# Two 128x64 column tiles in place of two zero-padded 128x128 matmuls for the last key tile of an attention kernel

## The chip, the cores and the metric

The kernel runs on one core of a Trainium2 chip. The metric is the device time of one execution in microseconds (us). A core has a matrix engine (PE, with its weight loads shown apart as PEld), a vector engine (DVE), an activation engine (ACT), a general engine (POOL), a queue engine (SP) and 16 DMA engines. A matmul on PE is two instructions: LDWEIGHTS puts the stationary operand into the 128x128 array, MATMUL streams the moving operand through it, one column after another, and writes PSUM.

## What is computed

Attention with RMS-normalized queries and keys, and then a layer-norm MLP with a residual. Eight batches, twelve heads, 448 tokens, head size 64:

```python
q_n, k_n = (rmsnorm(q, g_q), rmsnorm(k, g_k))
scores = scale * np.matmul(q_n, k_n.transpose(0, 1, 3, 2))
attn = np.exp(scores - np.max(scores, axis=-1, keepdims=True))
attn = attn / (np.sum(attn, axis=-1, keepdims=True) + 1e-09)
x = np.matmul(attn, v)            # 12 heads side by side: 768 columns
xn = (x - mu) / np.sqrt(var + 1e-06) * g_ln
out = x + np.maximum(xn @ w_ch1, 0.0) @ w_ch2     # 768 -> 3072 -> 768
```

## The kernel before

**Pairs and key tiles.** The kernel works on pairs of heads: 8 batches with 6 pairs each, 48 pairs. A head's 448 keys are three tiles of 128 and a rest of 64. For a pair that gives seven key tiles: tiles 0 to 2 are of the first head, 3 to 5 of the second, and tile 6 holds the last 64 keys of both heads. Scores are laid out with keys on the partitions and the 448 queries along the free dimension, so that their exponentials can serve at once as stationary operands of the product with V.

**The contraction.** A key is split into a high and a low half-precision part. Both stand along the contraction (64 rows high, 64 rows low, together 128), and the query is there twice. So every score matmul contracts over all 128 rows of the array, also that of tile 6.

**Scores** (`scores(p, i)`). For i below 6 one matmul (L351) loads 128 keys as weights and streams 448 query columns of that head. For tile 6 the transposed keys of a pair stand in a buffer `left` of 192 columns: 64 keys of the first head, 64 zeros, 64 keys of the second head. Two matmuls (L354, L355) write the same 128x448 tile of PSUM: the first takes columns 0 to 127 (keys of the first head and zeros) with the first head's queries, the second takes columns 64 to 191 (zeros and keys of the second head) with the second head's queries and adds to it. Then ACT takes the exponential of the whole tile (L357). Score tiles have two PSUM buffers (three in the later part).

**Values** (`values(p, i)`). Each exponential tile is used as weights, in four matmuls (three at L389, one at L391), over 65 columns of V (a column of ones gives the sum), or over 130 columns for tile 6. After tile 6, DVE divides and evacuates (`evac_o`, L404 to L411).

**The MLP** runs batch by batch, one batch behind the attention: `up` (L631, six matmuls of up to 512 columns for each of 24 hidden tiles, evacuated by ACT at L633) and `down` (L647, 24 matmuls of 384 columns for each output tile, evacuated by DVE at L651).

**The order.** Each engine executes its own list in order. For the first batch the order is a list by hand (`ORDER`: S3.6 is the scores of tile 6 of pair 3). Afterwards `run_rest` takes the chunks of the MLP of batch b and puts steps of the attention of batch b+1 between them in proportion to their cost, so that score, value and MLP matmuls alternate on PE. The order on PE, ACT, POOL and SP is as emitted; that on DVE is left to a scheduler in `run_rest`. Inputs are loaded ahead by DMAs; from the ninth load unit on the normalized keys and queries are transposed by DMA (L257 to L270), before that by PE (L312 to L329). The low part of the keys is made on DVE at L239.

**One other small tile.** Once, in the last batch, `flag` sums a check over the partitions with a matmul of one weight column in 32-bit floats (L760, tile psF, two passes). In the built program it is the only matmul of the kernel before that is marked as a tile smaller than 128x128: 128x32. It is emitted behind the third `up` of the last batch, between ordinary 128x128 matmuls.

Of the kernel before, what the change touches and what calls it, by code (L numbers as in the profile page):

```python
# [16 lines left out]
ts = bass.ts  # L17

B, H, S, D = 8, 12, 448, 64
# [56 lines left out]
class _Fast:  # L76
# [261 lines left out]
    def scores(self, p, i):  # L338

        nc = self.nc  # L340
        c = self.prs[p]
        q, left = c["q"], c["left"]
        if i == 0:
            c["E"] = self.p_e.tile([128, 7, S], FP16, tag="E", name="E")
        if p > UNIT_PAIR[DMA_UNIT] and (7 * p + i) % 3 == 2:
            ps = self.ps_tr.tile([128, 512], FP32, tag="tr", name="psS3")
        else:
            ps = self.ps_s.tile([128, 512], FP32, tag="psS", name="psS")
        if i < 6:
            h = i // 3  # L350
            nc.tensor.matmul(ps[:, 0:S], c["main"][:, ts(i, 128)], q[:, ts(h, S)],  # L351
                             start=True, stop=True)
        else:
            nc.tensor.matmul(ps[:, 0:S], left[:, 0:128], q[:, 0:S], start=True, stop=False)  # L354
            nc.tensor.matmul(ps[:, 0:S], left[:, 64:192], q[:, S:2 * S], start=False, stop=True)  # L355
        g = self.group(p, i)
        nc.scalar.activation(out=c["E"][:, i], in_=ps[:, 0:S], func=AFT.Exp,  # L357
                             scale=self.units[PAIR_UNIT[p][0]][3][:, g:g + 1], bias=EXP_BIAS)

        u = PAIR_UNIT[p][0]  # L360
        if i == 6 and UNIT_PAIR[u] == p and u > 4:
            self.least(u)
# [584 lines left out]
```

## Time and profile before

| what | value |
|---|---|
| median of three runs | 608.54 us (608.29 to 608.70) |
| span of the profiled execution, first to last instruction | 606.9 us |
| PE busy with matmuls | 579.4 us, 4500 recorded matmuls |
| mean granted TensorE clock | 0.996 |
| L354 and L355, 48 matmuls each | 17.2 and 17.1 us busy, 358 and 357 ns mean |
| L351, 288 matmuls of the same shape | 100.9 us busy, 358 ns mean |
| L760, its two passes | 0.2 us busy, 164 ns mean |

The profile comes from one execution. Matmuls are pipelined: a record of 0.35 us covers a matmul from its start until its last result is out, while the next one may start much earlier. What a matmul costs a busy PE is the distance from its start to the next start, which the timeline shows. "Idle before" is the time that an engine stood still before an instruction, with what ended it. The chain of waits is followed back from the last instruction of the program; a line's share of it is how much of the span that line itself set.

### The profile page before, as it was taken

The numbers are of one execution on the slowest core, as the hardware profiler recorded it, in microseconds if no ns is written. First come the engines' busy times: TensorE is split into PE (matmuls) and PEld (weight loads), VectorE is DVE, ScalarE is ACT, GpSimd is POOL, SyncE is SP. The second block draws the span as 40 slices with busy tenths as digits, with TensorE's granted clock in tenths as the row PEclk, the third lists the DMA queues.
The fourth block names the chain that finished last, engine by engine and source line by source line (L and its number), as shares of the span: only waits on it lengthen the run. The fifth ranks groups of instructions, "written<-read, shape, count | busy, mean of one in ns | idle before, by whom it ended". The sixth has DMA issues, their size and how long they took to land.

```text
span 606.9 us, 11525 instructions
## 1 busy us (share of the span) xinstructions
PE 579.4 (95%) x4500; PEld 346.4 (57%) x4500; DVE 287.1 (47%) x643; ACT 359.5 (59%) x673; POOL 190.1 (31%) x245
## 2 busy tenths in 40 slices
PE   2887999999999999999999999999999999999995
PEld 1555666655566666655566666655566666654564
DVE  5799567734256256715256255633356322530011
ACT  5996887268743697458753598538754377124200
POOL 3854432233541355332552345423412000000000
PEclk9899999999999999999999999999999999999999
DMA  8999999478954596747955485748733330030011
GB/s 225 275 192 200 214 225 187 103 211 83 149 157 107 89 136 154 174 133 90 126 129 127 114 123 141 188 120 124 125 74 68 92 62 1 31 100 0 1 53 57
DMA packets 130861, 75.29 MB, mean 124 GB/s; under 512 B 96656, under 2 KB 121040, under 8 KB 130800
## 3 DMA queue, kind: packets, MB, share of 16 engines
q1 hardware_dynamic: 114048, 45.12, 38.3%
q0 software_dynamic: 16080, 28.94, 22.1%
q8 instruction: 37, 0.61, 0.5%
q10 hardware_dynamic: 672, 0.43, 0.2%
q14 instruction: 24, 0.20, 0.1%
HBM read 52.36 MB, written 11.01 MB: 104 GB/s over the span
## 4 chain that ended last, share of the span: by engine, by line
PE 90%; DVE 2%; ACT 0%; issue 0%; DVEq 0%
PE psC L647 36%; PE psH L631 35%; PE psS L351 8%; PE oA L389 5%; PE oB L391 2%; PE psS L354 1%; PE psS L355 1%; PE tr L329 0%; PE tr L315 0%; PE psU L677 0%; DVE stat L555 0%; DVE xn L576 0%; DVE x L406 0%; DVE qU L334 0%; ACT E L357 0%
## 5 line engine op out<-in xcount | busy, mean ns | idle before, releaser
L631 PE MATMUL psH<-xnT,w 128*128 128x512 f16 (+1 forms) x1134 | 241.9, 353 | 0.0
L357 ACT ACTIVATE E<-psS,rr_all 128x448 f16<-128x448 f32 x336 | 207.6, 635 | 49.5 <-PE psS L351 44.3
L647 PE MATMUL psC<-w,hT 128*128 128x384 f16 (+1 forms) x1368 | 234.7, 323 | 0.0
L633 ACT ACTIVATE hT<-psH 128x512 f16<-128x512 f32 (+1 forms) x189 | 104.1, 551 | 124.3 <-PE psH L631 122.3
L647 PEld LDWEIGHTS <-hT 128*128 128x128 f16 x1368 | 127.8, 98 | 74.4
L631 PEld LDWEIGHTS <-w 128*128 128x128 f16 x1134 | 102.6, 98 | 80.5
L351 PE MATMUL psS<-qU,kU 128*128 128x448 f16 x288 | 100.9, 358 | 8.0 <-ACT E L357 5.3
L389 PEld LDWEIGHTS <-E 128*128 128x128 f16 x1008 | 71.2, 99 | 48.7 <-issue 4.1
L228 POOL TENSOR_TENSOR qkv<-qkv,gprod 128x896 f32<-128x896 f32 x21 | 43.7, 2080 | 95.3 <-issue 49.5
L389 PE MATMUL oA<-v,E 128*128 128x65 f16 x864 | 67.0, 194 | 0.1
L651 DVE SCALAR_TENSOR_TENSOR x<-psC,rs_all,x 128x384 f32<-128x384 f32 x48 | 28.9, 615 | 72.0 <-PE psC L647 71.5
L404 DVE RECIPROCAL rec_all<-oA 128x6 f32<-128x6 f32 x48 | 9.3, 193 | 94.0 <-PE oA L389 93.8
L391 PE MATMUL oB<-v,E 128*128 128x65 f16 x288 | 52.0, 194 | 0.1
L127 POOL DMA_DIRECT2D qkv<-in_k_dram x14 | 11.2, 799 | 129.8 <-ACT E L357 60.3
L217 DVE TENSOR_REDUCE ssq<-khl 128x14 f32<-128x896 f32 (+1 forms) x24 | 25.6, 1065 | 44.6 <-ACT khl L214 44.5
L351 PEld LDWEIGHTS <-kU 128*128 128x128 f16 x288 | 28.2, 99 | 25.8 <-issue 6.1
L217 DVE TENSOR_REDUCE ssq<-qn 128x14 f32<-128x896 f32 (+1 forms) x25 | 26.1, 1046 | 21.9 <-ACT qn L214 21.8
L67 DVE SCALAR_TENSOR_TENSOR qn<-qkv,rr_all 128x256 f16<-128x256 f32 (+1 forms) x72 | 26.3, 424 | 15.3 <-ACT rr_all L221 15.3
L391 PEld LDWEIGHTS <-E 128*128 128x128 f16 x336 | 32.7, 97 | 0.3 <-DVE xl L411 0.2
L239 DVE TENSOR_TENSOR khl<-qkv,khl 128x896 f16<-128x896 f32 x21 | 22.7, 1083 | 10.6 <-ACT khl L236 9.7
L406 DVE TENSOR_TENSOR x<-oA,rec_all 128x384 f32<-128x384 f32 x48 | 26.8, 558 | 1.5
L555 DVE BATCH_NORM_STATS2 stat<-x 128x6 f32<-128x256 f32 (+1 forms) x75 | 26.2, 404 | 0.6
(104 smaller groups left out, 448.4 us busy)
## 6 DMA issues: line engine op xcount, KB each, us to landing
out_dram<-x SPq DMA_DIRECT2D x20, 384.0 KB, 2.5
qkv<-in_k_dram POOLq DMA_DIRECT2D x14, 384.0 KB, 3.9
qkv<-in_q_dram POOLq DMA_DIRECT2D x14, 384.0 KB, 5.2
qkv<-in_v_dram POOLq DMA_DIRECT2D x14, 384.0 KB, 7.8
w<-in_moe_w_ch_dram POOLq DMA_DIRECT2D x3, 1536.0 KB, 12.6
w<-in_moe_w_ch_dram POOLq DMA_DIRECT2D x2, 2304.0 KB, 24.1
qkv<-in_k_dram SPq DMA_DIRECT2D x7, 384.0 KB, 6.6
qkv<-in_q_dram SPq DMA_DIRECT2D x7, 384.0 KB, 6.1
```

The costliest lines, as they stand in the source:

```text
L67: nc.vector.scalar_tensor_tensor(out=out, in0=x, scalar=8.0, in1=r.unsqueeze(2).broadcast_to([x.shape[0], g, D]), op0=ALU.mult, op1=ALU.mult)
L217: nc.vector.tensor_reduce(out=c["ssq"][:, n], in_=c["sq", n], axis=AX.X, op=ALU.add)
L228: (nc.vector if u in DVE_KG else nc.gpsimd).tensor_tensor(out=c["t"][1], in0=c["t"][1], in1=sh.gprod.unsqueeze(1).broadcast_to([128, g, D] ...
L351: nc.tensor.matmul(ps[:, 0:S], c["main"][:, ts(i, 128)], q[:, ts(h, S)], start=True, stop=True)
L357: nc.scalar.activation(out=c["E"][:, i], in_=ps[:, 0:S], func=AFT.Exp, scale=self.units[PAIR_UNIT[p][0]][3][:, g:g + 1], bias=EXP_BIAS)
L389: nc.tensor.matmul(oA[:, t, cs], E[:, i, ts(t, 128)], rhs, start=(i == 0 and t == 0), stop=(i == 6 and t == 2))
L391: nc.tensor.matmul(oB[:, cs], E[:, i, 320:448], rhs, start=(i == 0), stop=(i == 6))
L406: nc.vector.tensor_tensor(out=x[:, :, 128 * hp:128 * hp + 128].rearrange("p t (e d) -> p t e d", e=2), in0=oA[:, :, :, 0:D], in1=rec[:, 0: ...
L631: nc.tensor.matmul(ps[:, 0:N], sh.w1[:, dc, ts(f, 128)], xnT[:, dc, 0:N], start=(dc == 0), stop=(dc == NDC - 1))
L633: nc.scalar.activation(out=hT[:, f, 0:N], in_=ps[:, 0:N], func=AFT.Relu)
L647: nc.tensor.matmul(ps[:, 0:g[1]], hT[:, f, ts(t, 128)], sh.w2[:, f, cols], start=(f == 0), stop=(f == NFF - 1))
L651: nc.vector.scalar_tensor_tensor(out=x[:, cols], in0=ps[:, 0:g[1]], scalar=self.rs[:, b, t:t + 1], in1=x[:, cols], op0=ALU.mult, op1=ALU.add)
```

## The change

For tile 6 each head now has a matmul of its own with 64 weight columns. The first takes the 64 keys of the first head and writes partitions 0 to 63 of the PSUM tile; the second takes the 64 keys of the second head and writes partitions 64 to 127. Nothing accumulates, and the zeros in `left` are no longer read (they are still written).

```diff
         else:
-            nc.tensor.matmul(ps[:, 0:S], left[:, 0:128], q[:, 0:S], start=True, stop=False)
-            nc.tensor.matmul(ps[:, 0:S], left[:, 64:192], q[:, S:2 * S], start=False, stop=True)
+            for e in range(2):
+                nc.tensor.matmul(ps[64 * e:64 * e + 64, 0:S], left[:, 128 * e:128 * e + 64],
+                                 q[:, ts(e, S)], start=True, stop=True)
```

In the built program the two weight loads and the two matmuls of each pair are marked as tiles of 128x64 of the array, the first at column 0, the second at column 64; all other matmuls keep their marks. The lists of PE, ACT, POOL and SP hold the same instructions in the same order. On DVE the scheduler moves a few instructions: at three places in the stretch that it orders, the low part of a unit's keys (L239 of the kernel before) comes behind the evacuation of a pair (L404 to L411) and three statistics (L555) instead of ahead of them, and one evacuation of the MLP (L651) comes behind all of these; in a fourth place a small reduction (L366) comes two instructions later.

## The prediction, made before the changed kernel ran

> **What bounds the kernel now.** I read the page's busy times and chain first, then busy times by stage, then the chain by line.
>
> ```profile
> PE 579.4 (95%) x4500; PEld 346.4 (57%) x4500; DVE 287.1 (47%) x643; ACT 359.5 (59%) x673; POOL 190.1 (31%) x245
> ...
> PE 90%; DVE 2%; ACT 0%; issue 0%; DVEq 0%
> ```
>
> ```profile
> 0.00:58.00 58.00, 37.78 (x430) 25.75 (x431) 45.74 (x94) 44.73 (x86) 31.13 (x41) 0.97 0.98 232
> ...
> 120.00:520.00 400.00, 399.87 (x3045) 235.52 (x3043) 179.30 (x413) 255.70 (x477) 139.74 (x186) 1.00 0.61 119
> ```
>
> The first column after a stretch's length is PE. From 120 to 520 us PE is busy in 399.87 of 400 us at full clock; ACT, next, in 255.70. Only in the first 58 us does PE stand still for long (20 us). So a change of PE's work counts in full after 58 us, and in part before. Where are the edited matmuls?
>
> ```profile
> 0.00:58.00 58.00, 2.72 (x7) 0.77 (x7) 0.97 0.98 232
> 58.00:520.00 462.00, 14.45 (x41) 4.00 (x41) 1.00 0.66 126
> ```
>
> ```profile
> by line: PE psC L647 35.8%; PE psH L631 35.1%; PE psS L351 7.7%; PE oA L389 5.0%; PE oB L391 1.7%; PE psS L354 1.3%; PE psS L355 1.3%; PE tr L329 0.4%; PE tr L315 0.4%; PE psU L677 0.4%; DVE stat L555 0.4%; DVE xn L576 0.3%; DVE x L406 0.3%
> ```
>
> The first view is L354 alone: 41 of its 48 matmuls lie in the dense stretch. In the chain L354 has 1.3% of 606.9 us, 7.9 us; L355 the same.
>
> **What the old pair costs.** One pair in the dense stretch, PE and then its weight loads:
>
> ```profile
> 294.11 0.35 PE L354 MATMUL psS<-qU,kU 128*128 128x448 f16 x1
> 294.30 0.35 PE L355 MATMUL psS<-qU,kU 128*128 128x448 f16 x1
> 294.49 0.33 PE L389 MATMUL oA<-vl,E 128*128 128x130 f16 x3
> ```
>
> ```profile
> 293.89 0.10 PEld L354 LDWEIGHTS <-kU 128*128 128x128 f16 x1
> 294.11 0.10 PEld L355 LDWEIGHTS <-kU 128*128 128x128 f16 x1
> ```
>
> Start to start is 0.19 us each, so the pair costs 0.38 us. The reader is to see that each load starts one matmul ahead of its use (294.11 for the matmul of 294.30): loads are hidden. 7.9 us at 0.19 us is 41.5 matmuls, so about 41.5 pairs count.
>
> **What the change removes.** If both tiles stream at once, one of two streams goes: 0.19 us a pair, 7.9 us at most. No instruction goes: still two loads and two matmuls of 448 columns. The zeros cost nothing before and nothing now.
>
> **What it adds: changes of tile shape.** Each pair now takes the array from 128x128 to 128x64 and back. No row shows 128x64, but one place shows a change of shape, L760 (128x32, one column of 32-bit weights, two passes) among L631's matmuls. Narrow windows one after another:
>
> ```profile
> 541.63 0.38 PE L631 MATMUL psH<-xnT,w 128*128 128x512 f16 x1
> ...
> 541.93 0.09 PEld L760 LDWEIGHTS psF<-cnt,ones 128*1 128x1 f32 x2 [0.42 <-issue]
> ...
> 541.94 0.16 PE L760 MATMUL psF<-cnt,ones 128*1 128x1 f32 x1
> ...
> 541.96 0.16 PE L760 MATMUL psF<-cnt,ones 128*1 128x1 f32 x1
> ...
> 542.05 0.11 PEld L631 LDWEIGHTS <-w 128*128 128x128 f16 x2
> ...
> 542.06 0.39 PE L631 MATMUL psH<-xnT,w 128*128 128x512 f16 x1
> ```
>
> L631's matmuls of 512 columns follow each other in 0.215 us (six in 1.29 us in the chain). So the one of 541.63 has streamed at 541.845, yet L760 starts at 541.94: 0.095 us lost going in. Its load starts at 541.93, not a matmul ahead: it was not pulled over the change. What it needs had long been made (DVE's last sum of it ran at 536.5), so this is no wait for data. Coming back, the second pass starts at 541.96 and L631 at 542.06: 0.10 us, again with its load just before it. I take 0.195 us for the two changes of a pair. Bounds: zero, if 32-bit operands and not the shape made the gap, and the full 0.195.
>
> The Trainium skill, "TensorEngine Tiling (Array Packing)", Key Properties, says that a change of tiling mode, as against a change of tile, drains the array. The trace agrees, with 0.095 and 0.10 us at L760; by the rule the fp16 pair pays both, and none between its two tiles. The sum is the one taken here.
>
> **What it adds: loads no longer hidden, and the second tile's late start.** The nearest rows are those same loads: 0.01 us from load to matmul at 541.93 and 542.05, and 0.02 us from the first pass to the second. The upper bound is the 0.10 us of a whole load record. For 64 columns I take 0.025 for the first load and 0.025 for the second tile's lag, near the short rows since a matmul did start 0.01 us behind its load; bounds 0 and 0.10 each.
>
> The skill's page "TensorE: Matmul & The Clock Gate" (LDWEIGHTS) gives columns/1.2 ns, 53 ns for 64 columns, and its table of weight-path modes wants 128 columns for the fast load that 128-column weights get. With two such loads in the open the pair would cost 0.195 + 0.19 + 0.107 = 0.49 us, an estimate by that page, and the kernel 613.1 us. No row here has a load of 64 columns.
>
> **Sum.** New pair: 0.195 + 0.19 (one stream) + 0.05 = 0.435 us, against 0.38: +0.055 us. Times 41.5: +2.3 us. The span of 606.9 becomes 609.2; the median of the runs lies 1.6 us above the profiled span, and stays so: 608.54 + 2.3 = **610.8 us**. The other seven pairs, in the first 58 us, sit beside idle PE and could add at most 7 x 0.055 = 0.4 us.
>
> **What moves on DVE.** At three places in the stretch ordered by the scheduler the low part of the keys (1.09 us) goes behind an evacuation. I cost it at nothing. One of them before:
>
> ```profile
> 304.69 1.09 DVE L239 TENSOR_TENSOR khl<-qkv,khl 128x896 f16<-128x896 f32 x1 [0.80 <-DMA kU<-khl]
> 305.82 0.20 DVE L404 RECIPROCAL rec_all<-oA 128x6 f32<-128x6 f32 x1
> ...
> 307.62 0.62 DVE L651 SCALAR_TENSOR_TENSOR x<-psC,rs_all,x 128x384 f32<-128x384 f32 x1
> ```
>
> The keys would be ready some 2.5 us later, near 308.3, but the DMA transpose that reads them is issued at 314.05 on SP: 5.7 us of cover. The evacuation of psC comes some 0.8 us later; three buffers of that kind, each filled for over 24 x 0.16 = 3.9 us, cover it. Without cover the price would be 3 x 2.5 = 7.5 us at most. ACT's exponential waits only for the second matmul, as before; PE's list is unchanged.
>
> **Rivals.**
> 1. *The tiles do not stream together* (the change doesn't do what it says). Then the pair is 0.195 + 0.38 + 0.025 = 0.60 us, +0.22, times 41.5 +9.1 us: 617.7. With another 0.10 between the tiles, 621.8. For it: all matmuls of this trace go one after another. Against it: none of them leaves columns of the array free.
> 2. *No drain for fp16*, the other side: L760's gaps come from its 32-bit operands, loads are pulled ahead as at 293.89, and the pair costs 0.19 + 0.025 = 0.215 to 0.24 us, so -0.165 to -0.14: -6.8 to -5.8 us, **602.2**. For it: L760 is one event, and differs in type too. Against it: on the way back the load is fp16 with 128 columns and waits all the same. It decides once the two changes cost below 0.14 us together (0.38 - 0.19 - 0.05), instead of 0.195. The skill's span model (same clock-gate page, "Measured speedup vs the span model") has tiles starting 4 ns apart and would give this rival 0.194 us a pair; it counts no change of mode.
> 3. *Half a drain*: changes at 0.07 each give a pair of 0.38 us and no difference, 608.5.
>
> **How the numbers follow.** Forecast 0.55, rival 1 0.20, rival 2 0.15, rival 3 0.10. The forecast's own range, with loads and lag from 0.01 to 0.15 us in sum, is +0.6 to +6.4 us: 609 to 615. The range for 8 in 10 leaves out the far part of rival 2 and the double price of rival 1: 603.5 to 619.5. What can be told from no change is 0.2%, 1.2 us. Faster 0.16 (rival 2 and a little of 3); same 0.18 (most of 3, the forecast's low end); slower 0.66.
>
> **What would show it.** In the timeline of the changed kernel at a pair: the first tile about 0.095 us after the end of the stream before it, its load close ahead; the second tile within 0.02 to 0.1 us of the first (0.19 or more is rival 1); the next matmul about 0.29 us after the second tile's start. Loads that start a matmul ahead again would be rival 2. The prediction is wrong if either gap is below 0.05 us, if the second tile waits for the first, or if PE shows new waits in the dense stretch that come from DVE.

## The result, and the profile after

The changed kernel takes 610.6 us in the median of ten runs (609.81 to 612.24), the kernel before 609.22 us, also over ten runs. The ratio is 1.0026, 95% interval 1.0016 to 1.0037: 1.6 us slower, 1.0 to 2.3 (the medians themselves differ by 1.4). The profile of the changed kernel comes from an execution of 611.87 us, 1.3 us above its median; why, is seen below.

The page of the changed kernel, its busy times and its chain by engine:

```profile
PE 581.6 (95%) x4500; PEld 341.4 (56%) x4500; DVE 286.8 (47%) x643; ACT 359.2 (59%) x673; POOL 187.1 (31%) x245
...
PE 90%; DVE 2%; ACT 0%; issue 0%; DVEq 0%
```

Nothing changed hands: PE sets the end as before, and the other engines are as busy as before. The chain by line (line numbers behind the edit are one higher):

```profile
by line: PE psC L648 35.6%; PE psH L632 34.9%; PE psS L351 7.8%; PE oA L390 5.7%; PE psS L355 2.2%; PE oB L392 1.7%; PE tr L315 0.5%; PE tr L329 0.4%; PE psU L678 0.4%; DVE stat L556 0.4%; DVE xn L577 0.3%; DVE x L407 0.3%; DVE qU L334 0.2%
```

The two score lines of before had 2.6% of 606.9 us together, 15.8 us; the one line of after has 2.2% of 610.1, 13.4 us. But L390, the value matmul that comes right behind the tiles, went from 5.0% to 5.7%, 30.3 to 34.8 us. A share is rounded to 0.1%, 0.6 us, so these are rough; but what the tiles save shows at their line, what they cost mostly at the next one, and the cost is larger. One pair of the dense stretch, PE in three narrow windows and the weight loads in one wider window:

```profile
296.31 0.38 PE L632 MATMUL psH<-xnT,w 128*128 128x512 f16 x1
...
296.62 0.38 PE L355 MATMUL psS<-qU,kU 128*64 128x448 f16 x2
...
296.93 0.34 PE L390 MATMUL oA<-vl,E 128*128 128x130 f16 x3
297.12 0.22 PE L392 MATMUL oB<-vl,E 128*128 128x130 f16 x1
```

```profile
296.62 0.11 PEld L355 LDWEIGHTS <-kU 128*64 128x64 f16 x2 [0.42 <-issue]
296.93 0.17 PEld L390 LDWEIGHTS <-E 128*128 128x128 f16 x3 [0.20 <-issue]
```

Four things are to be seen. The 512 columns of the matmul at 296.31 have streamed at 296.525 (0.215 us), yet the tiles start at 296.62: some 0.095 us in which no column streams. Both tiles are in one record of 0.38 us, as long as one of them: they start 3 ns apart and stream together. The next matmul starts 0.31 us behind them, where a stream takes 0.19. And both weight loads sit right at their matmuls instead of one matmul ahead. In all 41 pairs of the dense stretch the three distances, by the unrounded start times, are the same within some ns. Going in, the tiles start 0.093 to 0.095 us later than the next matmul usually does (0.216 us behind one of 512 columns, 0.162 behind 384, 0.029 behind 65). Between the tiles it is 0.003 to 0.004 us, and 0.309 to 0.310 to the next start. The matmul behind that follows 0.011 us later than usual. Together: 0.094 + 0.003 + 0.309 + 0.011 = 0.417 us a pair, against 2 x 0.189 = 0.378.

41 x 0.039 = 1.6 us. The dense part as a whole agrees: from the first matmul of `up` to the last of `down`, by the first and last start in these groups (before, then after):

```profile
L631 PE MATMUL psH<-xnT,w x1134: 324/378/390, 58.4 to 569.0; 128*128 128x512 f16 x96, 128*128 128x384 f16 x93
...
L647 PE MATMUL psC<-w,hT x1368: 246/326/328, 91.3 to 600.4; 128*128 128x384 f16 x189, 128*128 128x192 f16 x7
```

```profile
L632 PE MATMUL psH<-xnT,w x1134: 324/378/389, 60.1 to 572.3; 128*128 128x512 f16 x96, 128*128 128x384 f16 x93
...
L648 PE MATMUL psC<-w,hT x1368: 246/326/328, 93.1 to 603.7; 128*128 128x384 f16 x189, 128*128 128x192 f16 x7
```

By the unrounded starts 542.06 us became 543.53, 1.5 us more. The rest of the 3.2 us between the two profiled spans lies ahead of 60.1 us, where this execution had a lower clock for longer. The busy times by stage of the changed kernel (the third number from the right is the granted clock):

```profile
0.00:20.00 20.00, 7.37 (x45) 4.33 (x46) 11.21 (x26) 12.81 (x26) 8.52 (x17) 1.00 0.93 247
20.00:40.00 20.00, 16.69 (x199) 11.27 (x199) 17.67 (x33) 18.70 (x34) 13.92 (x16) 0.91 0.97 213
40.00:60.00 20.00, 14.79 (x192) 10.92 (x191) 17.15 (x37) 13.53 (x29) 8.64 (x10) 0.91 1.02 216
```

In the profile of before the second stage had 0.91 too, but the third (40 to 58 us) had 1.00. The first two experiments test whether the early part belongs to the change.

### The profile page after: what moved, and what is told of

It reads as the page before. It is cut to its first block, busy times and chain, and to the rows that moved or that the text cites. A ratio compares the mean times of both kernels' runs of the same rounds, so it can differ in the third digit from the quotient of the medians.

```text
span 610.1 us, 11523 instructions
## 1 busy us (share of the span) xinstructions
PE 581.6 (95%) x4500; PEld 341.4 (56%) x4500; DVE 286.8 (47%) x643; ACT 359.2 (59%) x673; POOL 187.1 (31%) x245
## 4 chain that ended last, share of the span: by engine, by line
PE 90%; DVE 2%; ACT 0%; issue 0%; DVEq 0%
PE psC L648 36%; PE psH L632 35%; PE psS L351 8%; PE oA L390 6%; PE psS L355 2%; PE oB L392 2%; PE tr L315 0%; PE tr L329 0%; PE psU L678 0%; DVE stat L556 0%; DVE xn L577 0%; DVE x L407 0%; DVE qU L334 0%; DVE ssq L217 0%; DVE khl L239 0%
## 5 line engine op out<-in xcount | busy, mean ns | idle before, releaser
L390 PEld LDWEIGHTS <-E 128*128 128x128 f16 x1008 | 68.4, 99 | 49.4 <-issue 13.7
L390 PE MATMUL oA<-v,E 128*128 128x65 f16 x864 | 67.5, 195 | 0.1
L392 PEld LDWEIGHTS <-E 128*128 128x128 f16 x336 | 32.8, 98 | 0.3 <-DVE xl L412 0.2
L239 DVE TENSOR_TENSOR khl<-qkv,khl 128x896 f16<-128x896 f32 x21 | 22.7, 1080 | 8.2 <-ACT khl L236 6.6
```

The costliest lines, as they stand in the source:

```text
L390: nc.tensor.matmul(oA[:, t, cs], E[:, i, ts(t, 128)], rhs, start=(i == 0 and t == 0), stop=(i == 6 and t == 2))
L392: nc.tensor.matmul(oB[:, cs], E[:, i, 320:448], rhs, start=(i == 0), stop=(i == 6))
```

## The experiments

All times are medians, and the ratios are against runs of the kernel before on the same chip (medians 608.99 to 609.1 us). Differences from before are worked out from the ratio, if nothing else is said.

### Which pairs lose the time

```diff
         else:
-            nc.tensor.matmul(ps[:, 0:S], left[:, 0:128], q[:, 0:S], start=True, stop=False)
-            nc.tensor.matmul(ps[:, 0:S], left[:, 64:192], q[:, S:2 * S], start=False, stop=True)
+            if p >= 7:
+                for e in range(2):
+                    nc.tensor.matmul(ps[64 * e:64 * e + 64, 0:S], left[:, 128 * e:128 * e + 64],
+                                     q[:, ts(e, S)], start=True, stop=True)
+            else:
+                nc.tensor.matmul(ps[:, 0:S], left[:, 0:128], q[:, 0:S], start=True, stop=False)
+                nc.tensor.matmul(ps[:, 0:S], left[:, 64:192], q[:, S:2 * S], start=False, stop=True)
```

This is the edit of the first run; the second has `if p < 7`. Tiles in the dense stretch alone:

> Tiles only for the 41 pairs from pair 7 on (VectorE's order as in the changed kernel). Theory, from the changed kernel's trace: a pair costs 0.42 us instead of 0.38 (two changes of shape at 0.095, a load in the open, one stream saved), 41 x 0.04 = +1.7 us over before, ratio about 1.0027: all of the change's loss. Rival, the loss comes from the seven early pairs, where the profiled execution was already 1.8 us late: no difference from before, within 0.4 us.

610.41 us, ratio 1.0025 (1.0015 to 1.0034): +1.5 us, the whole loss. In its profile the dense part runs from 58.3 to 601.8 us, 543.52 us unrounded, as in the changed kernel, and it starts when it does in the kernel before:

```profile
L636 PE MATMUL psH<-xnT,w x1134: 323/378/389, 58.3 to 570.4; 128*128 128x512 f16 x96, 128*128 128x384 f16 x93
...
L652 PE MATMUL psC<-w,hT x1368: 246/326/328, 91.3 to 601.8; 128*128 128x384 f16 x189, 128*128 128x192 f16 x7
```

Tiles in the early pairs alone:

> Tiles only for the first 7 pairs (VectorE's order as before). Theory: PE has idle time there, so 0 to +0.3 us over before, ratio 1.000. Rival, the early pairs lie on a chain of their own and cost more: +1.8 us, ratio 1.003.

608.98 us, ratio 1.0001 (0.9992 to 1.001).

```profile
L636 PE MATMUL psH<-xnT,w x1134: 323/378/390, 58.2 to 568.8; 128*128 128x512 f16 x96, 128*128 128x384 f16 x93
...
L652 PE MATMUL psC<-w,hT x1368: 246/326/328, 91.1 to 600.2; 128*128 128x384 f16 x189, 128*128 128x192 f16 x7
```

The dense part has 542.06 us again, as in the kernel before, and it starts at 58.2 us although the early pairs have tiles. The early pairs cost nothing that can be measured, 0.6 us at most by the interval; the late start in the changed kernel's profile was that execution's own.

### What a change of tile shape costs by itself

A matmul of one column behind the padded pair, once as a 128x64 tile and once as an ordinary one. It writes a column of the score tile that nobody reads.

```diff
             nc.tensor.matmul(ps[:, 0:S], left[:, 64:192], q[:, S:2 * S], start=False, stop=True)
+            nc.tensor.matmul(ps[0:64, S:S + 1], left[:, 0:64], q[:, 0:1], start=True, stop=True)
```

```diff
             nc.tensor.matmul(ps[:, 0:S], left[:, 64:192], q[:, S:2 * S], start=False, stop=True)
+            nc.tensor.matmul(ps[:, S:S + 1], left[:, 0:128], q[:, 0:1], start=True, stop=True)
```

> The padded pair of before, and behind each pair one more fp16 matmul of a single column as a 128x64 tile, into an unused column of PSUM. Theory, a change of tile shape costs 0.095 us each way whatever the type: 0.19 for the two, 0.03 for its own slot and 0.03 for its load, 0.25 us a pair, times 41.5 = +10 us, about 619. Rival, the drain at L760 was due to its 32-bit operands: as the plain one, +1 us, about 610.

> The control: the same extra one-column matmul behind each pair, as an ordinary 128x128 tile. Both theories: its slot alone, 0.02 to 0.03 us a pair with its load hidden, +0.8 to +1.2 us, about 610. If the extra matmul itself were what costs, it would be +10 us here too.

As a tile: 618.44 us, ratio 1.016 (1.0144 to 1.0175), +9.7 us. As an ordinary matmul: 609.84 us, ratio 1.0018 (1.0008 to 1.0028), +1.1 us. So the same fp16 matmul of one column costs 8.6 us more (618.44 - 609.84) for its shape. The timelines, PE, with the tile and then with the ordinary one:

```profile
299.25 0.35 PE L355 MATMUL psS<-qU,kU 128*128 128x448 f16 x1
299.54 0.19 PE L356 MATMUL psS<-qU,kU 128*64 128x1 f16 x1
299.66 0.34 PE L390 MATMUL oA<-vl,E 128*128 128x130 f16 x3
```

```profile
282.89 0.35 PE L355 MATMUL psS<-qU,kU 128*128 128x448 f16 x1
283.08 0.17 PE L356 MATMUL psS<-qU,kU 128*128 128x1 f16 x1
283.11 0.33 PE L390 MATMUL oA<-vl,E 128*128 128x130 f16 x3
```

From 299.25 the padded matmul streams 0.19 us, to 299.44; then 0.10 us pass (0.094 by the unrounded starts), where the ordinary one follows at once. From the tile to the next matmul it is 0.123 us, where the ordinary one-column matmul has its successor after 0.028: 0.095 us more. The shape alone, with no 32-bit operand near, makes both gaps.

### What one stay in the shape holds

The two tiles done twice in a row.

```diff
-            for e in range(2):
+            for e in (0, 1, 0, 1):
                 nc.tensor.matmul(ps[64 * e:64 * e + 64, 0:S], left[:, 128 * e:128 * e + 64],
                                  q[:, ts(e, S)], start=True, stop=True)
```

> The changed kernel with each pair's two tiles done twice in a row (first, second, first, second), the result being the same. Theory, the two tiles stream side by side, and inside one stay in the 128x64 shape neither a drain nor a load is in the open: one more stream of 0.19 us a pair, 41.5 x 0.19 = +7.9 us over the changed kernel, about 618.5. If a load of 64 columns stays in the open each time (0.03): +9.1 us. If the tiles stream one after the other: 0.38 a pair, +15.8 us. If every tile paid a drain: 0.19 + 0.2 or more, +16 us or more.

617.65 us, ratio 1.0144 (1.0129 to 1.0158): +8.8 us over before, so some 7.2 more than the changed kernel's +1.6. The dense part of its profile has 551.10 us, 7.6 more than that of the changed kernel: near the +7.9 expected for one more stream a pair. Its timeline, narrow windows one after another, and its loads:

```profile
297.76 0.38 PE L632 MATMUL psH<-xnT,w 128*128 128x512 f16 x1
298.07 0.57 PE L355 MATMUL psS<-qU,kU 128*64 128x448 f16 x4
...
298.28 0.36 PE L355 MATMUL psS<-qU,kU 128*64 128x448 f16 x2
...
298.57 0.34 PE L390 MATMUL oA<-vl,E 128*128 128x130 f16 x3
```

```profile
298.06 0.14 PEld L355 LDWEIGHTS <-kU 128*64 128x64 f16 x4 [0.42 <-issue]
298.56 0.17 PEld L390 LDWEIGHTS <-E 128*128 128x128 f16 x3 [0.36 <-issue]
```

The second two start 0.21 us behind the first two, and the return takes 0.29 us from there. All four loads run within 0.14 us of the start: those of the second two are made ahead again. So the first stream takes 0.213 us by its start times, 0.024 more than the usual 0.189; the second 0.19, and then 0.096 of gap are left. That the 0.024 is the first load in the open is inferred and not shown by itself: the first matmul starts 0.002 us behind its load, the second load of the same tile starts 0.028 us behind the first one, and the second two tiles, with their loads ahead, don't pay it. Rival 1 of the prediction, one tile behind the other, would have shown 0.19 us between the first and the second tile.

### Paying once for two pairs

If the price is one for each stay, two pairs should share it. The last key tiles of two neighbouring pairs are put next to each other, behind the values of the pair before; the control does this with padded matmuls.

```diff
     def scores(self, p, i):
...
-        if i == 0:
+        if "E" not in c:
             c["E"] = self.p_e.tile([128, 7, S], FP16, tag="E", name="E")
...
     def attention(self):
...
-                if p < n and f"S{p}.{i}" not in done:
+                two = i == 6 and 8 <= p < n
+                if p < n and f"S{p}.{i}" not in done and not two:
                     c.append(lambda p=p, i=i: self.scores(p, i))
...
+                if two and p % 2 == 0:
+                    for o in range(2):
+                        c.append(lambda p=p + o: self.scores(p, 6))
```

In all versions with groups the third score buffer is given out by the new order of the scores. The control:

> The padded matmuls of before, but for pairs 8 and 9, 10 and 11, ... 46 and 47 the last key tiles of both pairs stand next to each other, behind the values of the pair before (control for the order alone). Both theories: PE does the same work in another order, within 0.5 us of before, ratio 1.000.

610.09 us, ratio 1.0013 (1.0004 to 1.0022), +0.8 us: a little more than expected, and its dense part has 542.80 us, 0.7 more than before. The order costs something by itself. Matmuls now wait for ACT to free a score buffer, as here, in its PE timeline:

```profile
77.78 1.14 PE L636 MATMUL psH<-xnT,w 128*128 128x384 f16 x6
79.15 0.35 PE L352 MATMUL psS<-qU,kU 128*128 128x448 f16 x1 [0.23 <-ACT E L358]
```

With tiles in the 20 groups:

> The same order, with tiles for the 20 groups of two pairs, and padded matmuls for the first 8 pairs. Theory, the two changes of shape are paid once for a group: 0.095 + 0.03 + 0.19 + 0.19 + 0.095 + 0.01 = 0.61 us against 0.76, -0.15 us a group, 20 x 0.15 = -3.0 us against its control, about 606, ratio 0.995. Rival, a drain is paid by each pair or tile: 0.84 us a group, +1.6 us.

607.07 us, ratio 0.997 (0.9958 to 0.9982): 1.8 us below before, and 3.0 us below its control by the two medians. That this is just the worked-out figure is in part luck: in the profiles the dense part is only 2.3 us shorter than the control's (540.51 against 542.80). One group:

```profile
304.39 0.22 PE L397 MATMUL oB<-vl,E 128*128 128x130 f16 x1
304.54 0.57 PE L357 MATMUL psS<-qU,kU 128*64 128x448 f16 x4
305.04 0.50 PE L657 MATMUL psC<-w,hT 128*128 128x384 f16 x2
```

The matmul of 130 columns usually has its successor after 0.057 us, here after 0.150: the gap going in is 0.093 again. The four tiles with their way back take 0.50. 0.093 + 0.50 + 0.01 = 0.61 us for two pairs, against 0.76 padded. But the first three groups, where the scores have two buffers, do not get this price. The second of them, PE in two windows and then ACT:

```profile
93.96 0.38 PE L357 MATMUL psS<-qU,kU 128*64 128x448 f16 x2
...
94.40 0.38 PE L357 MATMUL psS<-qU,kU 128*64 128x448 f16 x2
```

```profile
93.72 0.63 ACT L363 ACTIVATE E<-psS,rr_all 128x448 f16<-128x448 f32 x1
```

The second two tiles start 0.44 us behind the first two instead of 0.21, 0.05 us behind the end of the exponential (94.35) that frees a buffer. In the other two of these groups it is the same, with 0.32 and 0.45 us.

Groups only where there are three score buffers (the diff above with 14 in place of 8):

> As the grouped tiles, but groups only from pair 14 on, 17 of them, where the scores have a third PSUM buffer; padded matmuls in the order of before for pairs 0 to 13. Theory: 17 x 0.15 = -2.5 us against before, less the waits for the exponential that the late groups showed (0.3 us more each at 235 and 373 us in their profile): -2.0 us, about 607, ratio 0.997, no worse than the 20 groups, whose first three groups lost 0.4 us to such a wait. Rival, the gain of the 20 groups came from elsewhere than the shared changes of shape: no gain, ratio 1.000.

606.66 us, ratio 0.9959 (0.9947 to 0.9971), 2.5 us below before: faster than both kernels. Its 17 groups gain 17 x 0.15 = 2.55 us by the sums above. In its profile the dense part is 2.0 us shorter than in the kernel before (540.08 against 542.06), since PE waits 0.35 us for ACT at 234 and again at 372 us; so the median is as near to 2.55 by luck. The 20 groups had a further 3 x 0.15 to gain, but lost it to the waits inside those three groups. Whether the 0.4 us between the two medians is more than their spread stays open, as the intervals overlap.

## Why the prediction was right

**The total.** 610.8 was forecast, 610.6 measured; of +2.3 us forecast, +1.6 (1.0 to 2.3) came. The prediction's baseline was 608.54, the median over the ten runs of before is 609.22. That the totals agree to 0.2 us is luck: a baseline 0.7 us too low makes up for an addition 0.7 us too high. The difference says more. The profiled span, too, did not stay 1.6 us below the median: it came from an execution with a late start.

**The changes of shape, 0.195 us a pair:** right in place and size. 0.093 to 0.095 going in, and coming back 0.309 - 0.189 (the stream) - 0.024 (its longer first stream) = 0.096, which is also what the doubled pair shows behind its second stream. The doubt whether L760's 32-bit operands made its gaps is settled by the fp16 tile of one column and its control. By the rule of the Trainium skill ("TensorEngine Tiling (Array Packing)", Key Properties) the array drains at a change of mode and not between tiles of one mode. The traces agree: 0.094 and 0.096 us at the two changes, 0.003 us between the tiles of a pair, and no such gap inside the doubled pair and the late groups.

**One stream saved:** right. The tiles start 3 ns apart and the next matmul starts 0.31 us later, which leaves no room for a second stream of 0.19. The prediction expected it at 0.29; the longer first stream is the rest.

**Loads and lag, 0.05 us:** the term that was mis-sized. The lag of the second tile is 0.003 instead of 0.025 and below the 0.02 to 0.1 given as a sign. The first stream is 0.024 longer, as taken for the first load, and 0.011, which the sum left out, falls on the matmul after the return: 0.038 in sum. That makes the pair 0.417 instead of 0.435 and the loss +0.039 instead of +0.055. The Trainium skill ("TensorE: Matmul & The Clock Gate", LDWEIGHTS) puts a load at columns/1.2 ns, 53 ns for 64 columns. Here at most 0.024 us of the first load lies in the open, and nothing of the second tile's, so the estimate of 613.1 us by that page was too high.

**41.5 pairs, and nothing from the early ones:** right, by the two runs that split the pairs: 1.0025 and 1.0001.

**DVE's order at nothing:** right as far as the trace tells. At one of the three places of the changed kernel, DVE and then SP:

```profile
309.30 1.07 DVE L239 TENSOR_TENSOR khl<-qkv,khl 128x896 f16<-128x896 f32 x1
310.40 0.62 DVE L652 SCALAR_TENSOR_TENSOR x<-psC,rs_all,x 128x384 f32<-128x384 f32 x1
```

```profile
314.75 0.34 SPq L689 DMA_DIRECT2D out_dram<-x  x1
316.55 2.74 SPq L257 DMA_TRANSPOSE kU<-khl  x1
```

The keys are ready at 310.4 and read from 316.55: 6 us of cover left. Between 120 and 521 us no wait of PE for any engine is recorded, as before. The run with tiles in the dense stretch alone has this order, and its dense part is 1.5 us longer, where the pairs alone explain 1.6; that leaves DVE's order nothing. It was not tried alone with padded matmuls.

**The rivals.** One behind the other (617.7) falls by the 3 ns; no drain (602.2) by the one-column tile; half a drain (0.07 a change) by the 0.094 and 0.096. Against the first the prediction says that no matmul of the old trace leaves columns free; that overlooks L760, which has one weight column, but no number hangs on it.

## What to carry to other kernels

A column tile is worth its matmul time only if the stay in its shape is long: here a stay costs about 0.23 us (0.094 in, 0.003 between the tiles, 0.024 for the longer first stream, 0.096 out, 0.011 behind) and each pair of tiles saves one stream, 0.19 us for 448 columns. One pair loses 0.04 us, two pairs in a row gain 0.15, as long as the second pair does not wait for a buffer. Look for a rare instruction of another shape in the old trace: it prices the change before it is made, and then gather tiles of one shape before using them.

## What the runs showed of the hardware that was not expected

The gap going in does not depend on what went before: 0.092 to 0.095 us more than the usual distance behind matmuls of 65, 130, 384, 448 and 512 columns alike. And the second tile costs next to nothing, its load included: the two loads start 3 ns apart like the two matmuls, though no load was made ahead of the stay.
